# Linear attention with a gated layer: x of ten tiles turned by DMA transposes, stores in pairs on SyncE, weights in contiguous chunks, list of steps remade

## The chip, the cores and the metric

The kernel runs on one core of a Trainium2 chip. A time is that of one execution on the device, in microseconds (us); the kernel before has three runs. The span is the time from the first to the last instruction of one profiled execution on that core. The engines are TensorE (PE, with its weight loads PEld), VectorE (DVE), ScalarE (ACT), GpSimd (POOL) and SyncE (SP, which here only issues DMAs).

## The reference

q, k and v have 8 batches, 8 heads, 576 positions and 64 dimensions in float32. The attention has no matrix over positions: a 64 x 64 product of k and v per head takes its place.

```
q_s = exp(q - max_d q) / sum_d          # over the 64 dimensions
k_s = exp(k - max_s k) / sum_s          # over the 576 positions
kv  = k_s^T v                           # per batch and head, 64 x 64
x   = q_s kv                            # rows: 4608 = 8 x 576, columns: 512 = 8 heads x 64
H   = max(x w_h, 0)
T   = 1 / (1 + exp(-(x w_t + b_t)))
out = T H + (1 - T) x                   # 4608 x 512, float32
```

## The kernel before

The 4608 rows are cut into 36 tiles of 128 rows. Two batches make nine tiles: four of the first batch, four of the second, and one that holds the remaining 64 rows of both. The kernel computes exponentials without the maxima, and carries a column of ones beside v so that the sums come out of the same matmuls.

Every instruction stands in a list written out in the kernel, `ORDER`. A step is named by its kind, its tile or batch, and a part; `:A`, `:D` and `:P` choose ScalarE, VectorE or GpSimd. The list is played under a manual schedule: each engine gets its instructions in the list's order, and waits only for data and for buffers. An engine's queue is in order, SyncE's too: a DMA that waits for data holds up all DMAs behind it.

By batch the steps are: loads `k`, `v`, `q` (SyncE, 1.15 MB each from batch 2 on); `ek` and `eq` (exponentials on ScalarE to fp16); `vc` (v to fp16, ScalarE or GpSimd); `kv` (72 small matmuls a batch); `kr` and `kn` (reciprocals of the sums and the scaled kv, VectorE); `qt` (q turned by TensorE) and `qc` (its copy out of PSUM, VectorE or ScalarE).

By tile the steps are:

- `xu`: four matmuls (eight in every ninth tile) that give x without its scale, and the sums.
- `rs` (L340) and `x` (L346): reciprocals and the scaled x in fp16, VectorE.
- `xt` (L353): four TensorE transposes of 128 x 128, x to PSUM; `xe` (L360): the copy from PSUM to the tile xT, on ScalarE or VectorE.
- `bw`: the bias b_t into the gate's PSUM bank, by a ScalarE copy (L374) or by one matmul with ones (L376).
- `mt` (L384) and `mh` (L393): four matmuls each, xT with w_t and with w_h. Half of the identity has been taken off w_h / 2 (`whc`, `whd`), so that mh gives half of (H's argument - x).
- `th` (L408): tanh on ScalarE; `dd` (L412): d, VectorE; `uu` (L425): u = (tanh + 1) d, VectorE; `oo` (L442): o = u + x, GpSimd, or VectorE for parts of the last tile.
- In tiles whose `uu` has `:P` (4, 9, 22 and 26) GpSimd makes u = tanh d and, in `ee` (L417), e = d + x, and o is u + e.
- `st` (L451 to L455): the stores. Tiles go in pairs (`mate`), both o in one buffer of 4 KB a partition, stored by two DMAs of 64 partitions and 256 KB. Every ninth tile goes alone, and so do tiles 31 to 34, each by two DMAs of 128 KB. Tile 35 is cut into columns of 256, 128 and 128, with one store each, two of them issued by ScalarE.

Buffers that matter: xT has 5 (`xtp`), x 8 (`xp`), the pairs of o 7 (`op`, shared with the weights' landing tiles), the single o 5 (`o1p`, tag o1, shared with the landing of b_t). `turned` is the one PSUM bank for x's transposes. `fill` steps are matmuls on zeros that keep TensorE running through waits at the start.

The weights land two chunks of 128 rows at a time, each partition with two neighbouring rows (one run of 4 KB):

```
src.rearrange("(c p t) n -> p c (t n)", p=P, t=2)[:, c // 2]
```

so chunk n of the contraction is every second of 256 columns of x (`dims`), and `xt` reads x with a step of two.

Of the kernel before, what the change touches and what calls it, by code (L numbers as in the profile page):

```python
# [16 lines left out]
b_0 b_32 setuppool fill_16_turned setupdve v_0_0 q_0_0 k_0_0 k_0_2 v_0_2 w_h_0 bsplit w_h_2 vc_0_1:A w_t_0 vc_0_0:D
fill_4_turned bp bc w_t_2 eq_0_0 v_1_2 eq_0_1 fill_14_xu_0_0 qt_0_0 k_1_2 qc_0_0 ek_0_1 ek_0_0 ek_0_2 k_1_0
fill_7_xu_0_0 kv_0_0 ek_0_3 kr_0_0 kn_0_0 vc_0_2:A vc_0_3 q_1_0 fill_5_xu_0_0 xu_0_0 eq_0_2 rs_0_0 fill_1_xu_0_1
kv_0_1 x_0_0 bw_0 whc_0 qt_0_1 kr_0_1 half qc_0_1:A kn_0_1 v_1_0 whd_1 fill_3_xu_0_1 xu_0_1 whc_2 bw_1 xu_1_0 xt_0_0  # L20
rs_0_1 whd_0 xe_0_0 rs_1_0 x_0_1 v_2_0 wtc_0 fill_2_mh_0_0 mh_0_0 x_1_0 xt_0_1 whd_3 fill_1_qt_1_0 xu_2_0 whd_2 mt_0_0
xe_0_1:D rs_2_0 wtc_2:D xt_1_0 mh_0_1 xe_1_0 x_2_0 mt_0_1 mt_1_0 dd_0 k_2_0 th_0_0 xt_2_0 uu_0_0 xu_3_0 th_1_0 mh_1_0
rs_3_0 xe_2_0 x_3_0 bw_2:A mh_2_0 dd_1 ek_1_3 mt_2_0 ek_1_2 vc_1_3 oo_0_0 vc_1_2 q_2_0 uu_1_0 dd_2 xt_3_0 bw_3 th_2_0
kv_1_1 xe_3_0:D ek_1_1 uu_2_0 mt_3_0 ek_1_0 kr_1_1 kn_1_1 mh_3_0 th_3_0 k_3_0 eq_1_0 dd_3 oo_1_0 oo_2_0 fill_4_qt_1_0
qt_1_0 uu_3_0 vc_1_0:A vc_1_1 bw_4 qc_1_0 eq_1_1 oo_3_0 fill_1_xu_4_0 kv_1_0 v_3_0 kr_1_0 fill_1_xu_4_0 qt_1_1 kn_1_0
qc_1_1:A fill_1_xu_4_0 xu_5_0 xu_4_0 rs_5_0 vc_2_2 rs_4_0 x_5_0 bw_5:A fill_2_xu_4_1 qt_0_2 eq_1_2 x_4_0 fill_1_xu_4_1
xt_5_0 qc_0_2:A xu_6_0 q_3_0 vc_2_0:A xu_4_1 qt_1_2 ek_2_2 k_4_0 v_4_0 q_4_0 xe_5_0:D rs_4_1 rs_6_0 mh_5_0 x_6_0
xt_4_0 qc_1_2 mt_5_0 x_4_1 xe_4_0:D dd_5 xt_4_1 xu_7_0 th_5_0 mt_4_0 xe_4_1:D rs_7_0 ek_2_0 xt_6_0 mh_4_0 mt_4_1
mh_4_1 k_5_0 uu_5_0 x_7_0 xe_6_0:D kv_2_0 dd_4 mh_6_0 kr_2_0 kn_2_0 xt_7_0 dd_6 xe_7_0:D oo_5_0 bw_7:A th_4_0 eq_2_0
uu_4_0:P bw_6:A eq_2_1 qt_2_0 ee_4 xu_8_0 mt_6_0 ek_3_0 rs_8_0 oo_4_0 x_8_0 mt_7_0 th_6_0 qc_2_0 ek_3_2 xt_8_0 uu_6_0  # L30
xu_9_0 mh_7_0 rs_9_0 oo_6_0 eq_2_2 x_9_0 xe_8_0 qt_2_1 dd_7 th_7_0 xu_10_0 xt_9_0 bw_8:A mh_8_0 rs_10_0 vc_3_2 uu_7_0
vc_3_0:A x_10_0 mt_8_0 oo_7_0 dd_8 xe_9_0 kv_3_0 qc_2_1 th_8_0 bw_9:A xt_10_0 uu_8_0 qt_2_2 mh_9_0 eq_3_0 kr_3_0
xe_10_0:D st_5_0_1 oo_8_0 kn_3_0 mt_9_0 bw_10:A v_5_0 eq_3_1 dd_9 xu_11_0 mh_10_0 rs_11_0 ee_9 th_9_0 x_11_0 mt_10_0
eq_3_2 qc_2_2 dd_10 bw_11:A xt_11_0 xu_12_0 th_10_0 uu_9_0:P xe_11_0:D qt_3_0 q_5_0 ek_4_0 rs_12_0 mh_11_0 oo_9_0
x_12_0 uu_10_0 qc_3_0:A xt_12_0 mt_11_0 xe_12_0:D oo_10_0 dd_11 bw_12:A xu_13_0 th_11_0 qt_3_1 rs_13_0 st_1_0_0 vc_4_2
mt_12_0 x_13_0 qc_3_1:A st_1_0_1 uu_11_0 xt_13_0 xu_14_0 ek_4_2 k_6_0 mh_12_0 oo_11_0 rs_14_0 xe_13_0:D x_14_0 mh_13_0
th_12_0 dd_12 bw_13:A xt_14_0 xu_15_0 vc_4_0 uu_12_0 xe_14_0 mt_13_0 eq_4_1 rs_15_0 v_6_0 x_15_0 mh_14_0 dd_13 th_13_0
kv_4_0 bw_14:A oo_12_0 uu_13_0 eq_4_2 qt_3_2 eq_4_0 xt_15_0 kr_4_0 mt_14_0 qc_3_2 kn_4_0 xe_15_0 st_3_0_1 bw_15 dd_14
xu_16_0 th_14_0 mt_15_0 st_3_0_0 rs_16_0 ek_5_2 x_16_0 qt_4_0 uu_14_0 xu_17_0 qc_4_0:A xt_16_0 mh_15_0 rs_17_0 q_6_0
x_17_0 th_15_0 qt_4_1 xe_16_0:D bw_16:A dd_15 xu_18_0 qc_4_1:A xt_17_0 mh_16_0 rs_18_0 xe_17_0:D x_18_0 ek_5_0 mh_17_0  # L40
uu_15_0 st_7_0_1 xu_19_0 eq_5_0 dd_16 st_5_0_0 mt_16_0 rs_19_0 q_7_0 x_19_0 eq_5_2 xt_18_0 qt_5_0 th_16_0 dd_17
bw_17:A oo_13_0 oo_14_0 vc_5_2 vc_5_0 kv_5_0 uu_16_0 qc_5_0:A mt_17_0 kr_5_0 xe_18_0:D bw_18:A kn_5_0 xt_19_0 mh_18_0
th_17_0 v_7_0 xe_19_0:D ek_6_2 uu_17_0 xu_20_0 mt_18_0 rs_20_0 dd_18 bw_19:A qt_5_2 x_20_0 mh_19_0 oo_15_0 oo_16_0
oo_17_0 th_18_0 eq_5_1 uu_18_0 xt_20_0 xu_21_0 st_7_0_0 mt_19_0 oo_18_0 rs_21_0 xe_20_0 bw_20:A th_19_0 vc_6_0 ek_6_0
qc_5_2 x_21_0 qt_5_1 dd_19 xu_22_0 xt_21_0 mh_20_0 rs_22_0 uu_19_0 x_22_0 mt_20_0 bw_21:A xe_21_0:D dd_20 xu_23_0
th_20_0 mh_21_0 rs_23_0 oo_19_0 vc_6_2 qc_5_1:A uu_20_0 xt_22_0 st_19_0_1 mt_21_0 x_23_0 xe_22_0 oo_20_0 k_7_0 dd_21
qt_4_2 st_14_0_0 xu_24_0 th_21_0 mh_22_0 rs_24_0 st_10_0_0 qc_4_2 bw_22:A uu_21_0 eq_6_0 xt_23_0 st_8_0_0 mt_22_0
x_24_0 oo_21_0 dd_22 bw_23:A kv_6_0 th_22_0 xe_23_0:D st_10_0_1 ee_22 eq_7_0 qt_6_0 kr_6_0 mh_23_0 kn_6_0 uu_22_0:P
eq_6_1 xt_24_0 qc_6_0 xu_25_0 mt_23_0 bw_24:A rs_25_0 x_25_0 eq_6_2 st_21_0_1 qt_7_0 xe_24_0 dd_23 xu_26_0 th_23_0
st_21_0_0 xt_25_0 vc_7_2:A mh_24_0 rs_26_0 st_17_0_0 uu_23_0 x_26_0 mt_24_0 xe_25_0 dd_24 bw_25:A xu_27_0 th_24_0  # L50
xt_26_0 oo_22_0 vc_7_0 mt_25_0 xe_26_0 mh_25_0 ek_7_0 st_12_0_0 st_16_0_0 th_25_0 st_14_0_1 qc_7_0 uu_24_0 rs_27_0
x_27_0 qt_6_1 dd_25 xu_28_0 xt_27_0 bw_26:A oo_23_0 oo_24_0 mh_26_0 rs_28_0 uu_25_0 st_23_0_1 ek_7_2 x_28_0 st_12_0_1
mt_26_0 oo_25_0 dd_26 eq_7_2 kv_7_0 xe_27_0:D th_26_0 ee_26 qc_6_1 eq_7_1 xt_28_0 mh_27_0 kr_7_0 kn_7_0 bw_27:A qt_7_1
bw_28:A dd_27 xu_29_0 xe_28_0 mt_27_0 rs_29_0 uu_26_0:P qc_7_1 mh_28_0 x_29_0 th_27_0 xt_29_0 uu_27_0 xu_30_0 xe_29_0
mt_28_0 rs_30_0 dd_28 bw_29:A mh_29_0 x_30_0 th_28_0 xt_30_0 uu_28_0 xu_31_0 xe_30_0 mt_29_0 rs_31_0 dd_29 bw_30:A
mh_30_0 x_31_0 oo_26_0 oo_27_0 oo_28_0 th_29_0 xt_31_0 uu_29_0 xu_32_0 xe_31_0 mt_30_0 st_28_0_0 dd_30 bw_31:A
st_19_0_0 rs_32_0 oo_29_0 qt_7_2 mh_31_0 x_32_0 th_30_0 st_16_0_1 uu_30_0 xt_32_0 st_28_0_1 xu_33_0 xe_32_0 mt_31_0
st_23_0_0 mh_32_0 th_31_0 bw_32:A qc_7_2 rs_33_0 dd_31 x_33_0 xt_33_0 uu_31_0 qt_6_2 xu_34_0 xe_33_0 mt_32_0 rs_34_0
dd_32 bw_33:A mh_33_0 x_34_0 th_32_0 qc_6_2 xt_34_0 uu_32_0 xu_35_0 xe_34_0 mt_33_0 rs_35_0 bw_34:A dd_33 mh_34_0
x_35_0 oo_30_0 st_30_0_1 oo_31_0 st_26_0_0 st_25_0_1 st_30_0_0 st_31_0_1 st_31_0_0 th_33_0 xt_35_0 uu_33_0 mt_34_0  # L60
xe_35_0:D bw_35_0:A dd_34 mh_35_0 th_34_0 oo_32_0 st_32_0_0 oo_33_0 st_32_0_1 st_25_0_0 mt_35_0 uu_34_0 st_33_0_1
# [6 lines left out]
def kernel(  # L68
# [127 lines left out]

    def load_w(e, w, c):
        src = dict(t=moe_w_t, h=moe_w_h)[w]  # L200
# [224 lines left out]


    def mate(i):
        return None if i % 9 == 8 or i >= LAST - 4 else i + 1 if i % 9 % 2 == 0 else i - 1  # L430
# [14 lines left out]
    def st(e, i, h, r):  # L445
        bs, jp = tiles[i]
        cs, rows = columns(i, h), slice(NP * r, NP * r + NP)
        eng = nc.scalar if e == "A" else nc.sync
        dst = out[bs[0] * S:(bs[-1] + 1) * S, cs].rearrange("(p j) n -> p j n", j=NJ)
        if mate(i) is not None:  # L450
            eng.dma_start(dst[:, 2 * (jp + r) - 2:2 * (jp + r)], T[f"oo{i - 1}"][rows])  # L451
        elif len(bs) == 1:
            eng.dma_start(dst[:, 4 * (jp // 2) + 2 * r + jp % 2], T[f"o{i}_{h}"][rows])  # L453
        else:
            eng.dma_start(dst[:, 8], T[f"o{i}_{h}"][:, 0:cs.stop - cs.start])  # L455

# [43 lines left out]
```

## Time and profile before

| what | value |
|---|---|
| median of 3 runs | 124.83 us (124.61 to 125.35) |
| the profiled execution | 124.86 us |
| its span | 122.9 us |
| TensorE busy with matmuls | 112.5 us (92%), 1392 |
| VectorE, ScalarE, GpSimd busy | 100.9, 96.3, 63.9 us |
| chain that ended last | PE 61%, DMA 23% |
| HBM read, written | 30.41 MB, 9.44 MB |

The page cuts the span into 40 slices of 3.07 us; a digit is the busy share of an engine in tenths. A group is all instructions of one line, engine and shape, with their number and time. A time line gives for each stretch the start, the duration and, in brackets, how long the engine had been idle and what ended that. "SPq" is SyncE's issuing of a DMA, not the transfer.

### The profile page before, as it was taken

The page shows a single profiled execution, that of the slowest core. Times are in us where ns is not written, and L with a number is a line of the kernel's source. Part 1 is how long each engine was busy: PE and PEld are TensorE (multiplying, and loading weights), DVE is VectorE, ACT ScalarE, POOL GpSimd, SP SyncE. Part 2 cuts the span into 40 slices and gives each one's busy share as a digit, 9 for nine tenths or more (in the row PEclk, how much of TensorE's full clock was granted, in tenths as well). Part 3 has the DMA queues.
Part 4 walks back from the last instruction along what each step waited for, and adds up shares of the span by engine and source line. Part 5 has one row for each costly group of instructions (what it writes and reads, how often), then busy time and mean ns, then how long its engine had stood idle before and what let it go on. Part 6 is the DMA issues. An engine that isn't in the chain of part 4 may idle for free.

```text
span 122.9 us, 3478 instructions
## 1 busy us (share of the span) xinstructions
PE 112.5 (92%) x1392; PEld 65.7 (53%) x1392; DVE 100.9 (82%) x239; ACT 96.3 (78%) x150; POOL 63.9 (52%) x66
## 2 busy tenths in 40 slices
PE   5999999999999999999999999999999999999200
PEld 4645545445556665665566656566665655655100
DVE  5802899977989999989999999999999999998510
ACT  4279456887899999999999999899999687774200
POOL 5000102845328684988538547969739564464500
PEclk9999999999999999999999999999999999999995
DMA  3999999999999999999999999999989305988842
GB/s 119 382 403 402 412 387 391 392 395 381 389 392 388 392 389 388 392 386 402 392 401 396 395 400 403 393 400 395 402 275 249 76 0 108 237 277 264 203 113 87
DMA packets 17077, 40.08 MB, mean 326 GB/s; under 512 B 1187, under 2 KB 1571, under 8 KB 17061
## 3 DMA queue, kind: packets, MB, share of 16 engines
q1 hardware_dynamic: 16768, 39.65, 90.8%
q8 instruction: 11, 0.18, 0.6%
q10 hardware_dynamic: 292, 0.20, 0.5%
...
HBM read 30.41 MB, written 9.44 MB: 324 GB/s over the span
## 4 chain that ended last, share of the span: by engine, by line
PE 61%; DMA 23%; SPq 3%; ACT 3%; POOL 2%; issue 2%; DVE 1%; DVEq 0%; POOLq 0%
PE tps L384 20%; PE gps L393 20%; DMA v<-in_v_dram 11%; DMA w32h<-in_moe_w_h_dram 8%; PE qps L304 6%; PE xu L331 6%; PE turned L353 6%; PE kv L263 4%; DMA out_dram<-o 3%; POOL o L442 2%; SPq L187 2%; SPq L453 1%; ACT eq L313 1%; ACT qe L291 1%; DVE u L425 1%
## 5 line engine op out<-in xcount | busy, mean ns | idle before, releaser
L442 POOL TENSOR_TENSOR o<-u,x 128x512 f32<-128x512 f16 (+1 forms) x32 | 36.2, 1132 | 30.4 <-DVE u L425 27.2
L384 PE MATMUL tps<-w16t,xT 128*128 128x512 f16 (+2 forms) x152 | 37.1, 368 | 0.0
L393 PE MATMUL gps<-w16h,xT 128*128 128x512 f16 x144 | 36.9, 379 | 0.1
L346 DVE TENSOR_TENSOR x<-xu,rs 128x512 f16<-128x512 f32 (+1 forms) x38 | 24.8, 657 | 0.5
L425 DVE SCALAR_TENSOR_TENSOR u<-tps,d 128x512 f16<-128x512 f32 (+2 forms) x34 | 22.3, 658 | 3.2 <-ACT tps L408 1.4
L412 DVE SCALAR_TENSOR_TENSOR d<-x,gps 128x512 f16<-128x512 f16 x36 | 24.2, 673 | 0.8 <-PE gps L393 0.7
L250 POOL CAST v<-v 128x1152 f16<-128x1152 f32 (+1 forms) x13 | 12.9, 996 | 19.5 <-DMA v<-in_v_dram 19.5
L408 ACT ACTIVATE tps<-tps 128x512 f32<-128x512 f32 (+2 forms) x34 | 18.8, 560 | 4.3 <-PE tps L384 4.0
L291 ACT ACTIVATE qe<-q 128x1024 f16<-128x1024 f32 (+1 forms) x24 | 19.7, 839 | 0.8 <-DMA q<-in_q_dram 0.8
L393 PEld LDWEIGHTS <-xT 128*128 128x128 f16 x144 | 12.8, 98 | 12.4 <-ACT xT L360 0.9
L384 PEld LDWEIGHTS <-xT 128*128 128x128 f16 x152 | 13.4, 98 | 11.2 <-issue 0.2
L244 ACT ACTIVATE ek<-k 128x1152 f16<-128x1152 f32 (+1 forms) x20 | 18.9, 968 | 0.5 <-DMA k<-in_k_dram 0.5
L374 ACT COPY tps<-ball 128x512 f32<-128x512 f32 (+1 forms) x31 | 18.0, 584 | 0.8 <-DVE u L425 0.8
L360 ACT COPY xT<-turned 128x512 f16<-128x512 f16 (+1 forms) x19 | 10.9, 574 | 4.7 <-PE turned L353 4.6
L331 PE MATMUL xu<-kvb,eq 128*128 128x130 f16 (+1 forms) x160 | 14.5, 224 | 0.1
L353 PE MATMUL turned<-idh,x 128*128 128x128 f16 x144 | 14.3, 220 | 0.0
L353 PEld LDWEIGHTS <-x 128*128 128x128 f16 x144 | 10.4, 98 | 6.9 <-DVE x L346 2.7
L304 PE MATMUL qps<-idh,qe 128*128 128x128 f16 x144 | 12.0, 219 | 0.2
L331 PEld LDWEIGHTS <-eq 128*128 128x128 f16 (+1 forms) x160 | 9.9, 100 | 3.7 <-DVE kvb L281 0.8
L304 PEld LDWEIGHTS <-qe 128*128 128x128 f16 x144 | 9.5, 98 | 4.1 <-ACT qe L291 0.8
L313 DVE COPY eq<-qps 128x1024 f16<-128x1024 f16 (+1 forms) x15 | 7.3, 488 | 4.1 <-PE qps L304 4.0
L313 ACT COPY eq<-qps 128x1024 f16<-128x1024 f16 (+1 forms) x9 | 8.5, 940 | 2.5 <-PE qps L304 2.5
...
## 6 DMA issues: line engine op xcount, KB each, us to landing
...
```

The costliest lines, as they stand in the source:

```text
L244: nc.scalar.activation(t[:, :, c:c + n].rearrange("p j c d -> p c j d"), T[f"k32{b}"][:, c:c + n].rearrange("p c (j d) -> p c j d", j=NJ), ...
L291: nc.scalar.activation(t[:, j0:j1].rearrange("p j c d -> p c j d"), T[f"q32{b}"].rearrange("p c (j d) -> p c j d", j=NJ)[:, :, j0:j1], AF.Exp)
L304: nc.tensor.matmul(t[:, (j - j0) % 2, 2 * kk:2 * kk + 2, (j - j0) // 2], T[f"qe{b}"][:, j, 2 * kk:2 * kk + 2].rearrange("p c d -> p (c d)" ...
L331: nc.tensor.matmul(dst, T[f"eq{b}_{jp // 2}"][:, jp % 2, n], kvb[b % NKV][:, hh, kk], start=True, stop=True, skip_group_check=True)
L346: nc.vector.tensor_mul(t[:, k0:k1], sums(i, k)[:, :, :, 0:64], T[f"rs{i}_{k}"][:, 0:k1 - k0].unsqueeze(3).to_broadcast([P, k1 - k0, 4, D]))
L353: nc.tensor.matmul(t[:, n], T[f"x{i}"][:, dims(n)], idh, is_transpose=True, start=True, stop=True, skip_group_check=True)
L384: nc.tensor.matmul(gate_bank(i, k if i == LAST else 0), T[f"xT{i}"][:, n], w16["t"][:, n, cs], start=False, stop=(n == 3), skip_group_chec ...
L393: nc.tensor.matmul(t, T[f"xT{i}"][:, n], w16["h"][:, n], start=(n == 0), stop=(n == 3), skip_group_check=True)
L408: nc.scalar.activation(src, src, AF.Tanh, scale=0.5)
L412: nc.vector.scalar_tensor_tensor(t, T[f"x{i}"], -0.5, T[f"gps{i}"], op0=ALU.mult, op1=ALU.max)
L425: nc.vector.scalar_tensor_tensor(t[:, 0:cs.stop - cs.start], gate_bank(i, h), 1.0, T[f"d{i}"][:, cs], op0=ALU.add, op1=ALU.mult)
L442: eng.tensor_add(t[:, 0:w], T[f"u{i}_{h}"][:, 0:w], T[f"{'e' if lifted(i) else 'x'}{i}"][:, cs])
```

## The change

- Tiles 24 to 33 have no `xt` and `xe`. A new step `xd`, on SyncE, turns x into xT by one DMA transpose of 128 x 512 fp16 (131,072 B), from SBUF to SBUF.
- The weights are loaded in chunks of 128 neighbouring rows, so `dims` is a plain slice, as a transpose by blocks needs it; a partition's two rows are two runs of 2 KB.
- Tiles 31 to 34 are stored in pairs too. All stores are issued by SyncE.
- `op` has 8 buffers instead of 7, `o1p` 3 instead of 5.
- The list is remade. In it eight tiles have u and e on GpSimd (6, 9, 10, 14, 16, 22, 25, 27), other evictions change engines, the loads of batch 0 come as v, k, k, v, q, and k_7, the last load, stands behind 6 stores instead of 9. The last part reads as shown at the end of the diff.

```
-    op = pool("op", 7)
-    o1p = pool("o1p", 5)
+    op = pool("op", 8)
+    o1p = pool("o1p", 3)
...
     def load_w(e, w, c):
         src = dict(t=moe_w_t, h=moe_w_h)[w]
-        nc.sync.dma_start(w32(w, c).rearrange("p t n -> p (t n)"),
-                          src.rearrange("(c p t) n -> p c (t n)", p=P, t=2)[:, c // 2])
+        nc.sync.dma_start(w32(w, c), src.rearrange("(c p) n -> p c n", p=P)[:, c:c + 2])
 
     def dims(n):
-        return slice(2 * P * (n // 2) + n % 2, 2 * P * (n // 2) + 2 * P, 2)
+        return slice(P * n, P * n + P)
...
+    def xd(e, i, k):
+        t = T[f"xT{i}"] = xtp.tile([P, 4, P], FP16, tag="xT", name=f"xT_{i}")
+        nc.sync.dma_start_transpose(t, T[f"x{i}"])
...
     def mate(i):
-        return None if i % 9 == 8 or i >= LAST - 4 else i + 1 if i % 9 % 2 == 0 else i - 1
+        return None if i % 9 == 8 else i + 1 if i % 9 % 2 == 0 else i - 1
...
-        elif len(bs) == 1:
-            eng.dma_start(dst[:, 4 * (jp // 2) + 2 * r + jp % 2], T[f"o{i}_{h}"][rows])
...
+mt_20_0 x_22_0 xe_21_0 dd_20 xu_23_0 qt_4_2 th_20_0 xt_22_0 rs_23_0 oo_17_0 qc_4_2 mh_21_0 bw_21:A x_23_0 xe_22_0
+uu_20_0 xu_24_0 eq_6_1 mt_21_0 rs_24_0 dd_21 mh_22_0 x_24_0 oo_18_0 vc_6_0 oo_19_0 vc_6_2 oo_20_0 th_21_0 bw_22:A
+xt_23_0 uu_21_0 kv_6_0 eq_6_0 dd_22 oo_21_0 mt_22_0 eq_7_0 kr_6_0 xe_23_0:D xd_24_0 st_7_0_1 kn_6_0 st_7_0_0 mh_23_0
+th_22_0 st_16_0_0 bw_23:A xu_25_0 st_10_0_0 qt_6_0 bw_24:A rs_25_0 mt_23_0 x_25_0 qc_6_0:A dd_23 xu_26_0 th_23_0
+qt_7_0 ee_22 uu_22_0:P vc_7_0 rs_26_0 xd_25_0 vc_7_2 mt_24_0 x_26_0 st_10_0_1 uu_23_0 xu_27_0 oo_22_0 mh_24_0 rs_27_0
+x_27_0 xd_26_0 oo_23_0 st_19_0_1 dd_24 xd_27_0 st_12_0_0 st_21_0_0 qc_7_0:A th_24_0 bw_25:A qt_6_1 ek_7_2 xu_28_0
+mh_25_0 rs_28_0 uu_24_0 ek_7_0 mt_25_0 x_28_0 bw_26:A dd_25 kv_7_0 th_25_0 qc_6_1 xd_28_0 eq_7_1 mh_26_0 kr_7_0
+st_19_0_0 kn_7_0 mt_26_0 eq_6_2 st_23_0_1 eq_7_2 dd_26 st_8_0_0 xu_29_0 th_26_0 mh_27_0 oo_24_0 ee_25 uu_25_0:P
+st_12_0_1 rs_29_0 bw_27:A x_29_0 st_23_0_0 qt_7_1 uu_26_0 xu_30_0 qc_7_1:A mt_27_0 rs_30_0 dd_27 xd_29_0 mh_28_0
+bw_28:A x_30_0 st_14_0_0 th_27_0 st_14_0_1 qt_6_2 xu_31_0 mt_28_0 rs_31_0 qc_6_2 xd_30_0 x_31_0 st_21_0_1 bw_29
+th_28_0 dd_28 xu_32_0 qt_7_2 mh_29_0 rs_32_0 oo_25_0 oo_26_0 ee_27 qc_7_2:A xd_31_0 st_16_0_1 mt_29_0 uu_28_0 x_32_0
+bw_30:A dd_29 xu_33_0 th_29_0 mh_30_0 uu_27_0:P oo_27_0 oo_28_0 rs_33_0 xd_32_0 uu_29_0 mt_30_0 st_26_0_0 x_33_0
+bw_31:A oo_29_0 mh_31_0 dd_30 th_30_0 xu_34_0 uu_30_0 xd_33_0 mt_31_0 st_28_0_1 rs_34_0 dd_31 bw_32:A mh_32_0
+st_25_0_1 th_31_0 x_34_0 st_25_0_0 mt_32_0 uu_31_0 dd_32 xt_34_0 xu_35_0 th_32_0 oo_30_0 st_30_0_1 st_17_0_0 mh_33_0
+bw_33:A uu_32_0 st_30_0_0 xe_34_0 rs_35_0 mt_33_0 bw_34:A dd_33 st_28_0_0 x_35_0 mh_34_0 oo_31_0 oo_32_0 th_33_0
+bw_35_1:A mt_34_0 uu_33_0 st_32_0_1 dd_34 oo_33_0 xt_35_0 st_32_0_0 bw_35_2 th_34_0 xe_35_0:D bw_35_0:A uu_34_0
+mh_35_0 oo_34_0 mt_35_0 dd_35 mt_35_1 mt_35_2 th_35_0 st_34_0_0 uu_35_0 th_35_2 th_35_1 oo_35_0:P st_34_0_1 uu_35_2
+uu_35_1 oo_35_2 oo_35_1 st_35_2_0 st_35_0_0 st_35_1_0
```

More of the change, by code (lines that the diff above doesn't have):

```diff
@@ L16 @@
 ORDER = """
[L17 to L61, printed above, removed]
@@ L62 @@
-bw_35_1 mt_35_1 dd_35 bw_35_2 oo_34_0 mt_35_2 st_33_0_0 th_35_1 th_35_0 th_35_2 st_34_0_0 st_34_0_1 uu_35_1 uu_35_0
-oo_35_1 uu_35_2 st_35_1_0:A oo_35_0 oo_35_2:P st_35_0_0:A st_35_2_0
+b_0 b_32 setuppool fill_16_turned setupdve v_0_0 k_0_2 k_0_0 v_0_2 q_0_0 w_h_2 bsplit w_h_0 vc_0_1 w_t_2 fill_4_turned
+bp ek_0_3 half w_t_0 ek_0_2 v_1_2 ek_0_1 vc_0_0:A ek_0_0 k_1_2 vc_0_3 vc_0_2:A bc k_1_0 fill_22_xu_0_1 bw_0 kv_0_0
+kv_0_1 kr_0_0 kr_0_1 eq_0_0 q_1_0 kn_0_1 kn_0_0 eq_0_1 fill_6_xu_0_1 qt_0_0 whc_2 bw_1:A qc_0_0 whd_2 v_1_0
@@ new lines @@
+fill_5_xu_0_1 xu_0_1 whc_0 xu_0_0 qt_0_1 rs_0_0 xu_1_0 rs_0_1 qc_0_1:A x_0_0 whd_1 xt_0_0 x_0_1 k_2_0 xe_0_0 whd_0
+xt_0_1 rs_1_0 whd_3 mh_0_0 xe_0_1 x_1_0 wtc_2 mh_0_1 wtc_0:D xt_1_0 xu_2_0 xe_1_0:D mt_0_0 rs_2_0 dd_0 mt_0_1 v_2_0
+mt_1_0 x_2_0 th_0_0 vc_1_3:A xu_3_0 uu_0_0 xt_2_0 th_1_0 mh_1_0 rs_3_0 xe_2_0:D oo_0_0 bw_2:A x_3_0 mh_2_0 eq_0_2 dd_1
+ek_1_2 q_2_0 mt_2_0 ek_1_3 uu_1_0 xt_3_0 dd_2 bw_3 th_2_0 xe_3_0:D vc_1_2 kv_1_1 ek_1_1 uu_2_0 mh_3_0 ek_1_0 kr_1_1
+kn_1_1 k_3_0 mt_3_0 eq_1_0 dd_3 oo_1_0 oo_2_0 th_3_0 fill_1_qt_1_0 qt_1_0 vc_1_0:A vc_1_1 uu_3_0 eq_1_1 qc_1_0
@@ new lines @@
+fill_3_xu_4_1 kv_1_0 oo_3_0 v_3_0 kr_1_0 eq_1_2 fill_1_xu_4_1 qt_1_1 kn_1_0 qc_1_1:A bw_4:A ek_2_0 q_3_0 ek_2_2 vc_2_0
+vc_2_2 v_4_0 k_4_0 q_4_0 q_5_0 v_5_0 k_5_0 st_1_0_0 xu_4_1 xu_5_0 rs_4_1 xu_4_0 rs_5_0 rs_4_0 x_5_0 qt_0_2 qc_0_2
+fill_1_bw_5 xt_5_0 x_4_0 qt_1_2 xu_6_0 bw_5 xe_5_0:D rs_6_0 x_4_1 mt_5_0 x_6_0 xt_4_0 xt_4_1 xu_7_0 th_5_0 xe_4_1:D
+rs_7_0 xe_4_0 x_7_0 mh_5_0 mh_4_0 dd_5 xt_6_0 mh_4_1 qc_1_2 xe_6_0 kv_2_0 eq_2_0 mt_4_0 mt_4_1 xt_7_0 qt_2_0 uu_5_0
+dd_4 kr_2_0 oo_5_0 kn_2_0 xe_7_0:D mh_6_0 xu_8_0 mh_7_0 bw_7:A th_4_0 eq_2_1 uu_4_0 qc_2_0 oo_4_0 bw_6:A eq_2_2 rs_8_0
@@ new lines @@
+dd_6 ek_3_0 mt_6_0 x_8_0 dd_7 xu_9_0 th_6_0 qt_2_1 rs_9_0 xt_8_0 x_9_0 bw_8:A mt_7_0 xe_8_0:D ek_3_2 qc_2_1 xu_10_0
+xt_9_0 mh_8_0 rs_10_0 th_7_0 xe_9_0:D x_10_0 vc_3_0:A mt_8_0 xt_10_0 qt_2_2 th_8_0 st_5_0_0 st_1_0_1 k_6_0 st_3_0_0
+st_3_0_1 uu_7_0 dd_8 bw_9:A ee_6 uu_6_0:P vc_3_2 oo_6_0 oo_7_0 kv_3_0 uu_8_0 xe_10_0 mh_9_0 kr_3_0 bw_10:A kn_3_0
+mt_9_0 eq_3_1 dd_9 xu_11_0 th_9_0 qc_2_2 mh_10_0 rs_11_0 eq_3_2 x_11_0 eq_3_0 mt_10_0 dd_10 xt_11_0 xu_12_0 th_10_0
+xe_11_0:D qt_3_0 bw_11:A rs_12_0 mh_11_0 x_12_0 bw_12:A vc_4_0:A qc_3_0 xt_12_0 mt_11_0 xe_12_0:D dd_11 xu_13_0
@@ new lines @@
+th_11_0 mt_12_0 oo_8_0 ee_9 uu_9_0:P oo_9_0 uu_10_0:P ee_10 rs_13_0 ek_4_0 x_13_0 qt_3_1 oo_10_0 uu_11_0 xt_13_0
+th_12_0 xu_14_0 mh_12_0 rs_14_0 qc_3_1:A oo_11_0 xe_13_0:D x_14_0 mh_13_0 bw_13:A dd_12 vc_4_2 ek_4_2 xu_15_0 qt_3_2
+xt_14_0 rs_15_0 mt_13_0 qc_3_2 x_15_0 xe_14_0 uu_12_0 kv_4_0 th_13_0 dd_13 oo_12_0 bw_14:A xt_15_0 mh_14_0 eq_4_0
+kr_4_0 uu_13_0 kn_4_0 mt_14_0 oo_13_0 bw_15:A xe_15_0 dd_14 xu_16_0 th_14_0 qt_4_0 rs_16_0 ee_14 mt_15_0 eq_5_1 x_16_0
+qc_4_0 xu_17_0 uu_14_0:P eq_4_1 v_6_0 xt_16_0 mh_15_0 rs_17_0 x_17_0 th_15_0 oo_14_0 qt_4_1 bw_16:A xe_16_0:D dd_15
@@ new lines @@
+xu_18_0 eq_5_0 xt_17_0 vc_5_0 mh_16_0 rs_18_0 xe_17_0:D x_18_0 ek_5_0 st_5_0_1 mh_17_0 uu_15_0 q_6_0 xu_19_0 qc_4_1
+ek_5_2 q_7_0 xt_18_0 mt_16_0 rs_19_0 x_19_0 bw_17:A qt_5_0 dd_16 eq_5_2 th_16_0 v_7_0 dd_17 xe_18_0 vc_5_2 oo_15_0
+kv_5_0 ee_16 mt_17_0 kr_5_0 bw_18:A kn_5_0 uu_16_0:P eq_4_2 xt_19_0 mh_18_0 th_17_0 xe_19_0:D qc_5_0:A uu_17_0 xu_20_0
+oo_16_0 mt_18_0 dd_18 k_7_0 bw_19:A rs_20_0 qt_5_2 mt_19_0 x_20_0 th_18_0 ek_6_0 uu_18_0 xu_21_0 xt_20_0 mh_19_0
+rs_21_0 ek_6_2 th_19_0 bw_20:A qc_5_2 x_21_0 qt_5_1 xe_20_0:D dd_19 xu_22_0 mh_20_0 rs_22_0 uu_19_0 qc_5_1:A xt_21_0
@@ L463 @@
         wtc=wt_cast, whc=wh_cast, whd=wh_diag, ek=ek, vc=vc, kv=kv, kr=kr, kn=kn, eq=eq, qt=qt, qc=qc,
-        xu=xu, rs=rs, x=x, xt=xt, xe=xe, bw=bw, mt=mt, mh=mh, th=th, dd=dd, ee=ee, uu=uu, oo=oo, st=st)
+        xu=xu, rs=rs, x=x, xt=xt, xe=xe, xd=xd, bw=bw, mt=mt, mh=mh, th=th, dd=dd, ee=ee, uu=uu, oo=oo, st=st)
     with tc.manual_schedule():
```

## The prediction

> **What bounds the kernel now.** I read the slices first, then the stage table, then the groups of the transposes, then the end of the time lines.
>
> ```profile
> PE   5999999999999999999999999999999999999200
> DVE  5802899977989999989999999999999999998510
> ACT  4279456887899999999999999899999687774200
> POOL 5000102845328684988538547969739564464500
> DMA  3999999999999999999999999999989305988842
> ```
>
> TensorE is full from the second slice to slice 37. DMA is full to slice 29 and has holes afterwards. The stage table (us of each engine in five stretches) says what "full" is worth:
>
> ```profile
> 60.00:85.00 25.00, 25.00 (x347) 15.43 (x345) 24.07 (x55) 24.44 (x36) 17.11 (x16) 1.00 1.05 397
> 85.00:105.00 20.00, 20.00 (x231) 12.05 (x230) 18.95 (x40) 17.11 (x30) 12.57 (x12) 1.00 0.66 197
> 114.30:122.90 8.60, 0.00 (x0) 0.00 (x0) 1.54 (x6) 0.44 (x2) 1.16 (x2) 0.79 0.50 127
> ```
>
> From about 32 to 114.3 us the matmuls run without a gap at full clock: matmul time taken out there shortens the span one for one, as long as VectorE (18.95 of 20) and the others keep up. The last 8.6 us hold no matmul. The early part ends with a load: kv_1_0 begins at 28.30, just after v_1_0 lands at 27.50, and fills stand ahead of it. The same 13 loads lie in front of v_1_0 after the change, so I count nothing for the new start; it is covered by that load, and a later v_1_0 would cost its delay.
>
> ```profile
> L353 PE MATMUL turned<-idh,x x144: 218/219/232, 16.0 to 111.3; 128*128 128x128 f16 x144
> L353 PEld LDWEIGHTS <-x x144: 96/98/102, 16.0 to 111.3; 128*128 128x128 f16 x144
> ```
>
> 219 ns is one transpose alone; four follow each other in 0.223 us (the chain has "0.22 PE turned L353 x4" for most tiles). The tail:
>
> ```profile
> 113.89 0.39 PE L384 MATMUL tps<-w16t,xT 128*128 128x128 f16 x4
> 115.38 2.87 ACTq L455 DMA_DIRECT2D out_dram<-o  x2
> 117.38 0.42 DVE L442 TENSOR_TENSOR o<-u,x 128x256 f32<-128x256 f16 x1 [1.83 <-DMA out_dram<-o]
> 114.24 4.81 SPq L453 DMA_DIRECT2D out_dram<-o  x4
> 120.21 0.34 SPq L455 DMA_DIRECT2D out_dram<-o  x1
> ```
>
> The last o of tile 35 waits 1.83 us until a store has freed its o1p buffer, and SP's last stores wait for earlier landings (2.5 and 1.1 us in the waits of SP)[...]. The matmuls end at 114.25, the span at 122.9.
>
> [...] loads issued in mid-run land 12 to 13 us after their issue, the time of the backlog ahead. No run here shows a DMA transpose.
>
> **The change part by part.**
>
> *TensorE.* Tiles 24 to 33 lose four transposes each: 10 x 0.223 = 2.23 us. bw on TensorE in the dense stage goes from bw_15 (0.22) and two 128-wide ones (0.06 each) to bw_5, bw_29 (0.22 each) and one 128-wide: +0.16. Together -2.07 us. Fills after kv_1_0 fall from 5 to 2; they stand in waits, so nothing is counted.
>
> *The other engines.* ScalarE loses nine copies L360 (0.585 us each) of those tiles and VectorE one (0.41). ScalarE takes four evictions of q that VectorE had there; eight tiles instead of four have e and u on POOL (2.3 us more per tile for POOL, 0.69 less for VectorE). Summed over the list from mh_28 to mh_33 at the pitches of the time line (x 0.61, d 0.59, u 0.61, rs 0.13, POOL 1.15): VectorE 9.3, POOL 9.2, ScalarE 5.3 us beside 10.6 of TensorE. None becomes the bound, so the 2.07 us can be had.
>
> *What xd waits for and who waits for it.* SP issues xd_i only when x_i is written, and everything behind it on SP waits too: stores alone, as k_7 is the last load and stands ahead of xd_24. In the list TensorE has 3.45 us (tile 25) to 5.1 us (tiles 27, 28) of matmuls between the place of x_i and the first use of its xT; from xd_i itself 2.5 to 3.2 us. In that time must pass: x (0.69), the backlog on the ring, the transpose T, and the landing. A lone small store lands 1.5 us after its issue, 1.2 after the issue's end: I take 1.3 for the landing.
>
> Backlog. Stores of 256 KB land 0.62 to 0.64 us apart when they follow each other (87.78, 88.41, 89.02, 89.64). k_7 stands behind 6 stores instead of 9. Now v_7 landed at 82.92 as the end of 31.06 MB (23 loads, the weights, 7 stores); k_7 ends 31.98 MB (24 loads, the weights, 6 stores), so it lands near 85.2 at 396 GB/s, and the ring is free for xd_24 about 1 us earlier, at 84.2. [...] Between one xd and the next stand 4, 1, 1, 2, 5, 2, 1, 1, 1 stores: 18 x 0.64 = 11.5 us in the 20 us from xd_24 to mh_33.
>
> [...] Stall in sum: 0.5.
>
> Bounds on T. Below: 131,072 B at the pitch of the stores, 0.32 us; no stall less than 0, so nothing more is gained. [...] Walking the same ring with T = 0.85 gives stalls of 1.5 (tile 24) and 0.8 (tile 29), 2.3 in sum; with 1.3, 2.1 + 0.4 + 0.3 + 0.2 + 2.2 + 0.3 = 5.5; beyond that each us of T costs about 9. I [...] keep 0.32 to 1.7 for the range.
>
> *Tail.* With all of SP's stores in pairs, the o1p buffers of tile 35 were those of tiles 8, 17 and 26[...]. After the matmuls (now's clock): d_35 ends at 114.40; three u and two o on VectorE follow to 115.75; POOL's o_34 ends at 115.03. SP: two stores of 256 KB (0.54 each) to 116.2, then three of 0.35 to 0.4 to 117.3, landing by 118.5 to 119.3, plus the 1.14 us that now pass from the last landing to the end of the span: 119.7 to 120.4 instead of 122.9. I take -2.7. What is late next is SP's five issues in a row.
>
> *Weights.* 2 KB rows instead of 4 KB, the same 2.1 MB; the k, q and v loads move 390 to 400 GB/s with rows of 2,304 B. Nothing[...]. Moved stores: counted on the ring above.
>
> Sum against the profiled execution (span 122.9, 124.86 with what lies around it; the median of the three runs is 124.83): 124.86 - 2.07 - 2.7 + 0.5 = 120.6, and I add 0.4 for SP's unknown issue time of a transpose (a 256 KB store takes 0.47 to 1.2): **121.0 us**.
>
> **Rivals.**
>
> *The ring becomes the bound (slower).* If one transpose holds the ring for T above 1.2 us, SP's FIFO delivers xT later than the matmuls want it, tile by tile. At T = 1.2 the stalls (4.8) eat both gains: no change. At 1.7: 5.5 + 0.4 x 9 = 9.1, so 129.2. For it: [...] 18 stores between the transposes. Against it: the ring has 8.5 us spare in that stage[...].
>
> *Some stalls, tail gained.* T near 0.85, or SP's issue over 1 us: 124.86 - 4.8 + 2.3 = 122.4. Still faster.
>
> *The tail does not shorten.* Pairs to the last tile mean that half a MB waits for o_34; if it lands at the old pace, only the transposes count: 124.86 - 2.07 + 0.5 = 123.3. [...]
>
> *The start is later.* q_0 now lands fifth, not second, so the first x comes about 1 us later. Against it: the fills ahead of kv_1_0.
>
> **How the numbers follow.** A difference under 0.5% is about what a measurement of this kernel cannot tell from none: 124.2 to 125.5. T up to 0.6 and the tail gained: 0.30 (119.5 to 121.9). Some stalls or no tail gain: 0.23 (122 to 124.2). Near T = 1.2: 0.08. The ring as the bound: 0.39, over half of it up to 129.5. So faster 0.53, same 0.08, slower 0.39. For faster alone the range is 119.5 to 124; with the other sign it goes to 129.5.
>
> **What would show it.** Right: the group of x's transposes on TensorE has 104 (144 now); matmuls busy without gaps from tile 25 on; no wait of PE for a DMA over 0.5 us; matmuls end near 112.5; less than 7 us after them; no o of tile 35 waiting for a DMA. Wrong: TensorE idle before the matmuls of mt and mh, ended by the DMA of xT, about 2 us apart in every tile from 24 to 33, with transposes that land over 4 us after issue; or a long SP issue of each transpose; or a tail of 8 us again.

## The result, and the profile after

The kernel after takes 130.82 us (median of four runs, 130.53 to 131.5) against 125.02 us for the kernel before (four runs): a ratio of 1.047, interval 1.042 to 1.053. It is slower, where the forecast was 121.0 us. The profiled execution took 130.53 us, with a span of 128.8 us. In the runs below, a ratio leaves out executions that lie over 1.5% above the fastest of their kernel.

Line numbers have moved: in the kernel after, x's TensorE transposes are L350, `xd` is L362, `mt` L386, `mh` L395, the stores L453 and L455. The slices of the page are now 3.22 us wide:

```profile
PE   5999979997999999999999999998499629899800
DVE  5701889968899998989999999968488802887840
ACT  3164775998869999999999999999568401437310
POOL 4202001753465998995898978699386930454720
PEclk9999999999999999999999999999999986999995
DMA  4999999999999999999999999999999888989984
```

From slice 11 to slice 27 TensorE is full; the two slices of 7 tenths before that belong to the new start. From slice 28 on TensorE has the holes (4, 6, 2 tenths), and the row DMA, which had holes there before, is full to the last slices. The stage table of the kernel after (columns as before; the last two are the share of the DMA engines and GB/s):

```profile
85.00:105.00 20.00, 14.69 (x180) 8.01 (x177) 14.48 (x30) 13.22 (x21) 15.17 (x14) 1.00 0.95 212
122.40:128.80 6.40, 0.00 (x0) 0.00 (x0) 1.52 (x5) 0.43 (x2) 0.67 (x1) 0.76 0.66 200
```

From 85 to 105 us TensorE works 14.69 of 20 us, where it worked 20.00 before. The DMA engines are busy for 95% of it instead of 66%, and move 212 GB/s instead of 197: hardly more bytes for much more of their time. The tail after the last matmul is 6.4 us, 8.6 before. The groups on the page show where the time went:

```profile
L395 PE MATMUL gps<-w16h,xT 128*128 128x512 f16 x144 | 37.6, 387 | 6.7 <-DMA xT<-x 6.2
L350 PE MATMUL turned<-idh,x 128*128 128x128 f16 x104 | 10.2, 219 | 0.9 <-ACT xT L357 0.6
```

The 40 TensorE transposes are gone (104 for 144), and the matmuls of `mh` wait 6.2 us for the xT of the DMA; those of `mt` add 0.2. TensorE's time line shows where, in brackets the idle time before the group:

```profile
91.91 1.04 PE L395 MATMUL gps<-w16h,xT 128*128 128x512 f16 x4 [1.97 <-DMA xT<-x]
...
105.56 1.89 PE L395 MATMUL gps<-w16h,xT 128*128 128x512 f16 x4 [3.67 <-DMA xT<-x]
107.24 1.72 PE L386 MATMUL tps<-w16t,xT 128*128 128x512 f16 x4
...
111.36 1.04 PE L395 MATMUL gps<-w16h,xT 128*128 128x512 f16 x4 [0.44 <-DMA xT<-x]
```

Tile 25 waits 1.97 us, tile 29 3.67 us, and three others 0.17 to 0.44: 6.5 us. After the wait of 3.67 us the eight matmuls of tile 29 take twice as long, 1.89 and 1.72 us for four instead of 1.04 and less. SyncE's issues lead up to the wait of tile 29 (start, duration; `xd_28` is the first transpose, `xd_29` the second, `xd_30` the third):

```profile
94.69 2.22 SPq L362 DMA_TRANSPOSE xT<-x  x1
96.95 1.59 SPq L453 DMA_DIRECT2D out_dram<-o  x2
98.59 0.58 SPq L455 DMA_DIRECT2D out_dram<-o  x1
99.22 1.76 SPq L453 DMA_DIRECT2D out_dram<-o  x2
101.11 2.57 SPq L362 DMA_TRANSPOSE xT<-x  x1
103.72 1.22 SPq L453 DMA_DIRECT2D out_dram<-o  x2
105.06 2.19 SPq L362 DMA_TRANSPOSE xT<-x  x1
```

x_29 was written at 97.65 us. `xd_29` starts at 101.11, because SyncE was at the five stores ahead of it, its issue takes 2.57 us, and xT_29 lands at 105.5; TensorE had been ready at 101.9. Over the ten transposes (the landing is told for eight of them):

```profile
L362 SPq DMA_TRANSPOSE xT<-x x10: 1231/1588/2571, 81.4 to 112.4; - x10
DMA to landing us min/median/max: 2.8/3.5/5.4
```

(first line: minimum, median and maximum of the issue in ns, then the first and the last start). The last matmul ends at 122.36 us, 8.1 later than before; the tail gives 2.2 back; the span is 5.9 us longer.

### The profile page after: what moved, and what is told of

Same layout as the page of the kernel before. It is cut to its first block, busy times and chain, and to the rows that moved or that the text cites. A ratio compares the mean times of both kernels' runs of the same rounds, so it can differ in the third digit from the quotient of the medians.

```text
span 128.8 us, 3407 instructions
## 1 busy us (share of the span) xinstructions
PE 112.1 (87%) x1346; PEld 63.1 (49%) x1346; DVE 97.7 (76%) x232; ACT 92.2 (72%) x144; POOL 74.1 (58%) x75
## 4 chain that ended last, share of the span: by engine, by line
PE 55%; DMA 24%; DVE 7%; SPq 5%; ACT 2%; issue 1%; POOL 1%; DVEq 0%
PE gps L395 19%; PE tps L386 18%; DMA w32t<-in_moe_w_t_dram 10%; DMA xT<-x 10%; PE xu L328 5%; PE qps L301 5%; PE turned L350 4%; PE kv L260 4%; DMA out_dram<-o 3%; DVE u L427 3%; SPq L199 2%; DVE d L414 1%; SPq L186 1%; ACT tps L410 1%; SPq L453 1%
## 5 line engine op out<-in xcount | busy, mean ns | idle before, releaser
L444 POOL TENSOR_TENSOR o<-u,x 128x512 f32<-128x512 f16 (+1 forms) x28 | 31.8, 1137 | 33.8 <-DVE u L427 32.5
L395 PE MATMUL gps<-w16h,xT 128*128 128x512 f16 x144 | 37.6, 387 | 6.7 <-DMA xT<-x 6.2
L386 PE MATMUL tps<-w16t,xT 128*128 128x512 f16 (+2 forms) x152 | 37.5, 373 | 0.3 <-DMA xT<-x 0.2
L410 ACT ACTIVATE tps<-tps 128x512 f32<-128x512 f32 (+2 forms) x30 | 16.5, 554 | 14.5 <-PE tps L386 14.3
L427 DVE SCALAR_TENSOR_TENSOR u<-tps,d 128x512 f16<-128x512 f32 (+2 forms) x30 | 19.4, 653 | 3.8 <-ACT tps L410 3.2
L395 PEld LDWEIGHTS <-xT 128*128 128x128 f16 x144 | 12.4, 98 | 19.5 <-DMA xT<-x 7.9
L386 PEld LDWEIGHTS <-xT 128*128 128x128 f16 x152 | 13.9, 99 | 13.8 <-issue 1.3
L247 POOL CAST v<-v 128x1152 f16<-128x1152 f32 (+1 forms) x14 | 14.1, 1020 | 11.1 <-DMA v<-in_v_dram 11.1
L376 ACT COPY tps<-ball 128x512 f32<-128x512 f32 (+2 forms) x33 | 18.7, 573 | 2.2 <-DVE u L427 2.2
L419 POOL TENSOR_TENSOR e<-d,x 128x512 f16<-128x512 f16 x8 | 9.2, 1154 | 3.2 <-DVE d L414 3.1
L350 PE MATMUL turned<-idh,x 128*128 128x128 f16 x104 | 10.2, 219 | 0.9 <-ACT xT L357 0.6
L337 DVE RECIPROCAL rs<-xu 128x8 f32<-128x8 f32 (+1 forms) x38 | 7.5, 200 | 4.6 <-PE xu L328 4.3
L350 PEld LDWEIGHTS <-x 128*128 128x128 f16 x104 | 7.4, 98 | 4.8 <-DVE x L343 1.5
```

The lines of the kernel that those rows point to most:

```text
L350: nc.tensor.matmul(t[:, n], T[f"x{i}"][:, dims(n)], idh, is_transpose=True, start=True, stop=True, skip_group_check=True)
L376: nc.scalar.copy(t, ball[:, cs])
L386: nc.tensor.matmul(gate_bank(i, k if i == LAST else 0), T[f"xT{i}"][:, n], w16["t"][:, n, cs], start=False, stop=(n == 3), skip_group_chec ...
L395: nc.tensor.matmul(t, T[f"xT{i}"][:, n], w16["h"][:, n], start=(n == 0), stop=(n == 3), skip_group_check=True)
L427: nc.vector.scalar_tensor_tensor(t[:, 0:cs.stop - cs.start], gate_bank(i, h), 1.0, T[f"d{i}"][:, cs], op0=ALU.add, op1=ALU.mult)
L444: eng.tensor_add(t[:, 0:w], T[f"u{i}_{h}"][:, 0:w], T[f"{'e' if lifted(i) else 'x'}{i}"][:, cs])
```

## The experiments

Two theories were set against each other. **Issue**: SyncE, in order, spends so long on each transpose and each store that xT is asked for too late. **Ring**: the transfers of the stores and transposes together need more time than the stage has. Beside these stood the question what the other parts of the change, the tail above all, do alone.

### All ten tiles back to TensorE (e1_xt_back)

```
-... xd_24_0 st_7_0_1 ...
+... xt_24_0 xe_24_0:D st_7_0_1 ...      # the same for tiles 25 to 33; three copies on VectorE
```

> The changed kernel with xd of all ten tiles replaced by xt and xe again (three of the copies on VectorE, seven on ScalarE); stores, pools, weights and the rest of the list stay as changed. Theory (the DMA transposes alone cost the time, the rest of the change gains a little): no wait of TensorE for xT, matmuls end about 114.5 us, the tail is shorter than the 8.6 us of before, 122.5 to 123.5 us in all. Rival (the stores in pairs on one engine, the start or the weights cost it too): 126 or more, with the matmuls' end or the tail later than before.

Measured: 124.32 us (15 runs), ratio 0.994 (0.992 to 0.996), 6.5 us less than the kernel after. TensorE's holes are gone:

```profile
85.00:105.00 20.00, 19.51 (x236) 11.93 (x237) 16.51 (x37) 16.20 (x27) 15.41 (x14) 1.00 0.72 226
```

So the loss comes with the transposes; the list, the weights and the tail do not make it without them. But 124.32 us is more than the 122.5 to 123.5 of the theory. The matmuls end at 116.82 us, 2.5 later than before, and the tail is 5.7: the remade list, with its steps put back in these places, gives away most of what the tail gains. Which of its moves costs that was not taken apart.

### No stores in the stage (e2_no_stage_stores)

```
-... xd_24_0 st_7_0_1 kn_6_0 st_7_0_0 mh_23_0 ...
+... xd_24_0 kn_6_0 mh_23_0 ...          # the 18 stores between xd_24 and xd_33 left out
```

> The changed kernel without the 18 stores that stand between xd_24 and xd_33 (those rows of the output are not written). Theory (SyncE's in-order queue of issues and the ring behind it are shared by stores and transposes; a transpose alone keeps pace): from tile 26 on each transpose is issued within 0.3 us of its x, lands under 3.2 us after the start of its issue, TensorE waits for xT less than 1 us in all; 121 to 123 us. Rival (one transpose alone takes the ring or the issuing engine longer than a tile's matmuls, 2 us): the waits for xT stay over 4 us in all, 126 us or more.

Measured: 121.3 us (one run). The transposes and the stage in this kernel:

```profile
L360 SPq DMA_TRANSPOSE xT<-x x10: 1188/1192/1717, 81.4 to 103.5; - x10
DMA to landing us min/median/max: 2.4/2.4/3.4
```

```profile
85.00:105.00 20.00, 20.00 (x214) 10.99 (x212) 18.33 (x38) 15.25 (x25) 16.83 (x16) 1.00 0.41 61
```

A transpose without stores beside it costs SyncE 1.19 us and lands 2.4 us after its start; it goes as 512 packets of 256 B, with 0.78 us from the first to the end of the last (0.77 to 0.79 in seven of the ten). No matmul waits for it, and the matmuls end at 113.42 us. A transpose by DMA is thus no trouble by itself (121.3 us); with the stores beside it, it is (130.82).

### The stores issued by ScalarE (e3_stores_on_act)

```
-... xd_24_0 st_7_0_1 kn_6_0 st_7_0_0 ...
+... xd_24_0 st_7_0_1:A kn_6_0 st_7_0_0:A ...   # the same 18 stores
```

> The changed kernel with the 18 stores between xd_24 and xd_33 issued by ScalarE, at the same places of the list. Theory A (SyncE's time to issue is the limit: 1.2 to 2.6 us a transpose and 0.6 a store): the waits of TensorE for xT fall from 6.3 us to under 2, 123 to 126 us, with 0.5 us of ScalarE's time for each store. Rival B (the transfers on the 16 shared DMA engines are the limit): waits as they were, 129 to 132 us.

Measured: 131.35 us (four runs), ratio 1.050 (1.046 to 1.055): as slow as the kernel after. SyncE now has nothing but transposes:

```profile
L362 SPq DMA_TRANSPOSE xT<-x x10: 1193/1825/2938, 81.9 to 113.1; - x10
DMA to landing us min/median/max: 2.5/6.6/8.2
```

```profile
90.12 1.89 PE L386 MATMUL tps<-w16t,xT 128*128 128x512 f16 x4 [2.00 <-DMA xT<-x]
...
106.97 1.87 PE L395 MATMUL gps<-w16h,xT 128*128 128x512 f16 x4 [2.57 <-DMA xT<-x]
```

Six of the ten transposes are issued within 0.2 us of their x, and yet they land 6.6 us later in the median (of the seven whose landing is told), not 2.4. The time in the queue before the issue has become time after it. The time of rival B came true, its waits only in part: two of 2.00 and 2.57 us remain, 4.6 in all for 6.5 in the kernel after, but now both are followed by matmuls at half pace. Issue alone falls as a theory: taking the stores out of SyncE's way gains nothing while their bytes stay.

### Half of the transposes (e4_half)

```
-... rs_26_0 xd_25_0 vc_7_2 ...
+... rs_26_0 xt_25_0 xe_25_0 vc_7_2 ...   # tiles 25, 27, 29, 31 and 33
```

> The changed kernel with xt and xe for tiles 25, 27, 29, 31 and 33 and xd for 24, 26, 28, 30 and 32. Theory A (a queue that has to issue 2 stores and a transpose a tile, 2.7 us, against 2.05 us of matmuls; with half the transposes it needs 1.9): waits for xT under 1.5 us in all, 122 to 124 us. Rival B (each transpose is late by itself, from issue to landing): a wait of about 1 us or more in each of the five tiles, 126 to 128 us.

Measured: 126.02, 127.33, 128.09 and 128.46 us; ratio 1.013 (1.006 to 1.019), from the first two. The times lie in the range of rival B, but its mark, a wait in each of the five tiles, is missing. In the profiled execution, that of 128.09 us, there is one wait, 3.56 us before tile 30, whose transpose stands behind seven stores; the other four tiles wait for nothing, although the transposes still take SyncE 2.2 us in the median. With half the load, it seems, the place of a transpose in the queue decides; whether the faster executions have the same wait is not known.

### The same stores with an eighth of the bytes (f1_thin_stores)

```
+        if (i, r) in THIN and mate(i) is not None:
+            eng.dma_start(dst[:, 2 * (jp + r) - 2, 0:P], T[f"oo{i - 1}"][rows][:, 0, 0:P])
...
```

Each of the 18 stores carries 512 B a partition; a pair's carried 4 KB (the two stores of the single tiles 8 and 26 carried 2 KB).

> The changed kernel in which the 18 stores between xd_24 and xd_33 carry 512 B a row (1/8 of their bytes; the rest of those rows is not written), the same number of DMAs at the same places. Theory A (SyncE's issues, 0.6 us a store and 1.2 to 2.6 us a transpose, are the limit): TensorE still waits for xT over 3 us in all, 126 us or more. Theory B (the bytes of the stores on the ring, 1.2 us for 256 KB in this stage and not 0.64, are the limit): waits under 1.5 us in all, issue of a transpose near 1.2 us, 121 to 123 us, as without the stores.

Measured: 125.61 us (one run). The transposes, and SyncE before and at `xd_29`:

```profile
L362 SPq DMA_TRANSPOSE xT<-x x10: 1188/1200/1297, 81.5 to 107.5; - x10
DMA to landing us min/median/max: 2.4/2.4/3.2
```

```profile
94.66 1.58 SPq L455 DMA_DIRECT2D out_dram<-o  x2
96.29 0.63 SPq L457 DMA_DIRECT2D out_dram<-o  x1
96.97 1.99 SPq L455 DMA_DIRECT2D out_dram<-o  x2
99.08 1.24 SPq L362 DMA_TRANSPOSE xT<-x  x1
```

Without the bytes a transpose costs SyncE 1.20 us again and lands in 2.4. But the five stores still stand before `xd_29`, most of them 0.6 us each or more, and tile 29 waits 2.2 us, of 2.6 in all. The start of the last transpose, `xd_33`, tells the three kernels apart:

| kernel | `xd_33` starts, us | time, us |
|---|---|---|
| no stores in the stage | 103.5 | 121.3 (one run) |
| the stores' issues, an eighth of the bytes | 107.5 | 125.61 (one run) |
| the kernel after | 112.4 | 130.82 |

About 4 us of the loss come with the stores' issues in front of the transposes and about 5 with their bytes, as far as single runs can tell. The waits and the time lie between the two forecasts: both theories hold in part. With all bytes present the issues alone decide nothing (e3_stores_on_act), so the two parts are not independent.

### The stores spread evenly (f2_even)

```
-... xd_24_0 st_7_0_1 kn_6_0 st_7_0_0 ... st_16_0_0 ... st_10_0_0 ... xd_25_0 ...
+... xd_24_0 kn_6_0 ... st_7_0_1 st_7_0_0 xd_25_0 ...    # two between any two transposes
```

> The changed kernel with the same 18 stores in the same order, but spread evenly: two between each transpose and the next (instead of 4, 1, 1, 2, 5, 2, 1, 1, 1). Theory A (the ring has room, only the clump of five ahead of xd_29 and of four ahead of xd_25 is misplaced): the waits of 3.7 and 2.0 us go, 124 to 126 us. Theory B (the stage as a whole has more transfers than time, 18 x 1.2 + 10 x 0.9 = 31 us in 20): the waits move to other tiles, 5 us or more in all, 129 to 132 us.

Measured: 132.22 us (four runs), ratio 1.057 (1.053 to 1.061). From the waits of this kernel (us in total, times, longest):

```profile
PE gps L395 <- DMA xT<-x: 8.1, 8, 1.7
```

The long wait is gone, nothing exceeds 1.7 us, and the granted clock stays at 1.00 from 85 to 105 us; but nine of the ten tiles wait, 8.3 us in sum. So the five stores ahead of `xd_29` are not the cause but the place where the shortage shows. The stage as a whole is overfull: of the transfers or of SyncE's issues, this run alone cannot tell, since the order of the queue is all that it changes.

### Fills ahead of tile 29 (f3_fill29)

```
-... qt_7_2 mh_29_0 ...
+... qt_7_2 fill_16_mh_29_0 mh_29_0 ...
```

> The changed kernel with 16 matmuls on zeros (3.4 us) on TensorE ahead of mh_29, in the time in which it waits for xT of tile 29. Theory (the clock of TensorE falls after the idle 3.7 us, and the next eight matmuls take 3.2 us instead of 1.7): they take 1.7 us again, 128.5 to 129.5 us. Rival (the slow matmuls have another cause): no change, 130.5 to 131 us, or later if the fill outlasts the wait.

Measured: 131.27 us (four runs), ratio 1.050 (1.045 to 1.055); no gain. TensorE's time line in this kernel:

```profile
92.81 1.43 PE L395 MATMUL gps<-w16h,xT 128*128 128x512 f16 x4 [3.13 <-DMA xT<-x]
94.04 1.91 PE L386 MATMUL tps<-w16t,xT 128*128 128x512 f16 x4
...
104.09 3.62 PE L171 MATMUL gps<-blank 128*128 128x512 f16 x16
107.54 1.03 PE L395 MATMUL gps<-w16h,xT 128*128 128x512 f16 x4
108.41 1.03 PE L386 MATMUL tps<-w16t,xT 128*128 128x512 f16 x4
```

With fills in the wait the eight matmuls of tile 29 run at full pace, 1.03 us for four: the half pace does come from the idle time before. The time is that of the rival even so, because the gain went to two things: the fills outlast xT_29, which landed at 106.33, by 1.2 us, and in this execution tile 25 waited 3.13 us and was followed by the slow pace there.

### The tail alone (f4_before_tail)

The kernel before, with the new end only:

```
-    op = pool("op", 7)
-    o1p = pool("o1p", 5)
+    op = pool("op", 8)
+    o1p = pool("o1p", 3)
...
-        return None if i % 9 == 8 or i >= LAST - 4 else i + 1 if i % 9 % 2 == 0 else i - 1
+        return None if i % 9 == 8 else i + 1 if i % 9 % 2 == 0 else i - 1
...
-oo_35_1 uu_35_2 st_35_1_0:A oo_35_0 oo_35_2:P st_35_0_0:A st_35_2_0
+oo_35_1 uu_35_2 oo_35_0 oo_35_2:P st_35_1_0 st_35_0_0 st_35_2_0   # and no stores of tiles 31 and 33
```

> The kernel before with nothing of the change but the tail: tiles 31 to 34 stored in pairs, all stores by SyncE, op 8 and o1p 3 buffers, those steps moved accordingly at the end of its list. Theory [...]: the span ends about 6 us after the last matmul instead of 8.6, 122 to 123 us. Rival (the bytes that wait for o_34 then pass at the old pace): 124.5 to 125.5 us.

Measured: 122.72 us (six runs), ratio 0.980 (0.978 to 0.983), faster than both kernels. Its time line at the end:

```profile
115.61 0.41 DVE L442 TENSOR_TENSOR o<-u,x 128x256 f32<-128x256 f16 x1
...
116.41 2.24 SPq L455 DMA_DIRECT2D out_dram<-o  x3
```

The o that began at 117.38 after a wait of 1.83 us for a DMA begins at 115.61 and waits for none. The matmuls end at 114.42 us, for 114.27 before; the tail is 6.5 us.

### Three older stores moved ahead (g1_tail_early)

```
-... mt_30_0 st_28_0_0 dd_30 bw_31:A st_19_0_0 rs_32_0 ... st_16_0_1 ... st_23_0_0 ...
+... mt_30_0 st_19_0_0 st_16_0_1 st_23_0_0 st_28_0_0 dd_30 bw_31:A rs_32_0 ...
```

> The kernel of f4_before_tail with three stores (tiles 18/19, 15/16, 22/23, one half each), whose data is long there, moved ahead of the first store of tiles 27/28, for which SyncE waits 8.2 us with an idle ring. Theory (three stores of 1.2 us less on the ring in the last 12 us let the last stores be issued and land sooner): SyncE's last three issues take 0.4 us each instead of 0.75, 121.5 to 122.3 us. Rival (the end hangs on o_34 and the last matmuls alone): 122.5 to 122.9 us as f4_before_tail.

Measured, with the tail alone as its base: 122.63 us (five runs), ratio to the kernel before 0.980 (0.977 to 0.982), the same. SyncE's last three issues begin at 116.27 and take 2.24 us again; the two stores ahead of them were issued at 115.07, right after the o of tile 34. The end hangs on that o and on the issues behind it, not on the older stores.

## Why the prediction was wrong

**The step that failed is "Backlog", which priced the stores between the transposes, and with it the 0.4 us put down "for SP's unknown issue time".** Three terms were too small:

- *The stores' price.* 0.64 us for 256 KB was read from landings at 87.78 to 89.64 us, where the stores ran in the backlog behind the last load. Two stretches of each kernel show that this price does not hold in the stage of the transposes (each line ends with the share of the DMA engines and GB/s). The kernel before:

```profile
86.00:89.50 3.50, 3.50 (x34) 2.09 (x33) 3.23 (x7) 3.50 (x7) 2.32 (x3) 1.00 1.05 403
102.00:105.00 3.00, 3.00 (x29) 1.93 (x28) 2.90 (x7) 1.98 (x4) 1.21 (x2) 1.00 0.75 153
```

  and the kernel after, both stretches between the packets of two transposes:

```profile
86.50:88.70 2.20, 1.97 (x19) 1.09 (x16) 1.61 (x5) 1.71 (x4) 2.20 (x3) 1.00 1.04 416
94.70:97.20 2.50, 2.50 (x16) 1.25 (x15) 2.17 (x6) 2.08 (x5) 2.42 (x3) 1.00 1.00 187
```

  In the backlog the DMA engines moved 403 GB/s at a share of 1.05; later 153 at 0.75, which is 204 GB/s at full share. 262,144 B take 0.68 us at the first pace and 1.28 at the second (1.40 at the 187 GB/s of the kernel after). The trace of before held this number, in the stage in question: the 0.66 beside the 197 GB/s that the prediction quoted is 298 GB/s at full share, not 400. "The ring has 8.5 us spare" came from the wrong pace, and it is 20 - 11.5: the ten transposes were not taken off.
- *The transpose on the engines.* No run stood behind the time the prediction took for one; it was the author's estimate, and too small. Measured: 0.78 us from first to last packet without stores beside it, 168 GB/s. This is within the bounds kept (0.32 to 1.7) and would have cost little by itself.
- *The issue on SyncE.* 0.4 us in all; measured 1.19 us for one alone and 1.59 in the median, 2.57 at most, beside stores. The prediction knew that a store takes 0.47 to 1.2 us to issue but never summed this. With about 0.6 a store, as in the lines above, 18 x 0.6 + 10 x 1.19 = 22.7 us: by this estimate SyncE's issues alone are more than the stage of 20 us.

Put in its own sum: 18 stores at 1.3 and ten transposes at 0.78 make 31 us of the DMA engines in a stage of 20, where the prediction counted 18 x 0.64 = 11.5 for the stores. From the first to the last `xd` the kernel after takes 31.0 us (81.4 to 112.4), the kernel without those stores 22.1. The agreement is rough, since the first few stores still ran at the pace of the backlog, and some of the 31.0 us are SyncE's issues.

**The stalls.** "0.5 in sum" became 6.5, plus 1.5 for the half pace of tile 29 (eight matmuls in 3.23 us, from 105.56 to 108.79, for 1.73). The 0.5 was the author's estimate. Tile 24 waited 0.23 (k_7 landed at 86.57, not 85.2), and tile 29, whose xT landed at 105.5, waited 3.67. The passage and the landing are not what failed: from the end of its issue a transpose alone landed after 1.2 us, beside stores, from tile 26 on, after 1.5 to 2.0, where 1.3 was put down for the landing alone. The time went before that, in the queue and in the issue.

**The TensorE saving** of 2.07 us is there to be had: without the stores of the stage the matmuls run from 85 to 105 us without a gap, as the prediction said, and end at 113.42 us. The forecast was near 112.5. Of the 0.9 us between, 0.46 is a wait of the last tile for its copy of xT, and as much is a later start: kv_1_0 begins at 28.77 us instead of 28.30, where the prediction counted nothing (its rival "the start is later"). In the kernel after the 6.5 us of waits and the 1.5 of slow matmuls take the end from there to 121.4. Most of the 0.9 us up to the 122.36 measured is overlap that the waits undo: in the time line a group of matmuls begins about 0.16 us before the end of the one ahead of it (four at 88.23 last 1.02 us, the next begin at 89.10), and each of the five waits loses that as well, 0.8 us in all.

**The tail** was right in kind and nearly in size (the last o's wait of 1.83 us for a DMA and the waits of 2.5 and 1.1 us of SyncE's last stores for earlier ones are gone in the kernel after): 2.2 us in the kernel after, 2.4 by the tail alone (median against median), for 2.7 forecast. The missing part is SyncE's last three issues, 2.24 us together where 0.35 to 0.4 each were put down. No other engine became the bound, as said.

**The rivals.** The one on the other side, the ring as the bound, came true in its sign and near its 129.2 us, and its mark was seen, TensorE idle before `mh` and ended by the DMA of xT. Its cause was put in the wrong place: T above 1.2 us was wanted, T was 0.78, and the stores and the issues filled the ring. The stalls did not come "tile by tile" but for the most part in two tiles, and tile by tile only when the stores were spread evenly. Its chance, 0.39, had been held down by the same spare time that the wrong pace made. The range, cut at 129.5, left out the upper part of that rival, which was worked out only to T = 1.7 with the stores at 0.64. The rival with some stalls named an issue of over 1 us, which came true as well, but gave it 2.3 us of stalls and 122.4 us.

One reading of the prediction is loose without a part in the sum: the 12 to 13 us of the loads hold from the end of their issue (from its start they are 13 to 16).
